# From step 28 on, the FFN's products on TensorE in a fixed order by pairs of steps

## The chip, the cores and the metric

One core of one Trainium2 chip runs the whole program. The metric is device time in microseconds; before, three runs gave a median of 957.44 us (956.3 to 957.57).

## What is computed

Attention of 8 batches, 8 heads, 576 positions and 64 channels, made of a coarse part and a narrow band, and then a feed-forward block over all 4608 tokens:

```python
x = np.ascontiguousarray(attn_out.transpose(0, 2, 1, 3)).reshape(B * S, H * D)   # 4608 x 512
h = x @ w_in                       # 512 x 2048
r = np.maximum(h, 0.0)
g = s * (r * r) + b
return (g @ w_out).astype(np.float32)   # 2048 x 512
```

The attention itself adds two softmaxes: `out_d`, of queries, keys and values averaged over groups of 4 positions, repeated 4 times, and `out_local`, where a position sees only those less than 4 away.

## The kernel before

**Tiles and steps of the FFN.** The tokens are cut into 18 blocks `t` of 256, the 2048 hidden channels into 8 pieces `p` of 256. A step is one pair `(t, p)`; the list `order` (L784 to L787) has all 144 of them. From index 24 on it goes block by block: `(3, 0)` to `(3, 7)`, then `(4, 0)` and so on. Step 28 is `(3, 4)`, step 143 is `(17, 7)`.

Operands are split into a high and a low part of type fp32r, and a product takes three matmuls: high by high, low by high, high by low. One step has

- 24 products with w_in (`products1`, L631): the weights `wi` are loaded into the array, `xh` and `xl` stream past, 256 columns each, into the PSUM bank `ph`. Even steps use bank 4, odd ones bank 6 from block 3 on (but for step 25);
- `upper` (L644 to L646) on ScalarE: Relu and Square in place in `ph`, then a cast to `gh`;
- `lower` (L651) on VectorE: `gl = ph - gh`. Then `ph` is free again;
- 12 products with w_out (`products2`, L705 to L707): `gh` or `gl` is loaded, `wo` streams past, 512 columns each. Six go into one bank, six into another; from block 3 on these are banks 0 and 1. The third of every three reads `gl`.

`gh` and `gl` have two buffers; from block 3 on a step with `p % 3 == 2` takes a buffer of its own, `gb`, instead. Behind a block's last step `evict` (L683) reads both banks on VectorE, scales, adds and stores (`os`), and only then may the next block's w_out products write there.

**Attention beside it.** The batches of attention run while the FFN works on earlier ones. Their products, transposes included (`sa`, `tp`, `tr`, `up`, `ot`), stand on TensorE between those of the FFN, most of their work on VectorE (L539, L558, L559), GpSimd (L537, L559) and ScalarE. `split_x` makes a block's `xh` and `xl` (L612, L613).

**What sets the order.** Up to step 28 a long text, `PLAN`, fixes each engine's order piece by piece; at its end the w_in and the w_out products of steps 0 to 27 are all issued. Behind it a loop (L913 to L925) takes one step after the other: its 24 w_in products, `upper` and `lower` with high priority, a share of attention (`advance`), then w_out products up to three steps back, and another share of attention. These are only priorities: a list scheduler decides what stands where on each engine, and w_out products slide between w_in products as it sees fit. For the first ten steps `behind_plan` keeps everything behind the plan's last instruction on its engine.

Each engine works through its own queue in order, so an instruction that waits holds up all behind it.

Of the kernel before, what the change touches and what calls it, by code (L numbers as in the profile page):

```python
# [20 lines left out]
B, H, S, D = 8, 8, 576, 64  # L21
# [65 lines left out]
def attention_ffn_kernel(ctx, tc, qk, vw_in, vr_in, vdm, qkn, vn, w_in, w_out, s_in, b_in, out):  # L87
    nc = tc.nc
# [21 lines left out]
    def bank(i, shape, name):  # L110
        return ps.tile(shape, F32, tag=f"k{i}", name=name)
# [488 lines left out]
    def split_x(t):  # L600
        tags = ("os", "xl2") if t == 2 else ("xh", "xl")
        xh, xl = (home[tag].tile([P, HP, TB], F32R, tag=tag, name=name)
                  for tag, name in zip(tags, ("xh", "xl")))
        t0 = t * TB
        while t0 < (t + 1) * TB:
            b = t0 // S
            while (b, HP - 1) not in complete:
                next(gen)
            n = min((t + 1) * TB, (b + 1) * S) - t0
            src = xt[b][:, :, t0 - b * S : t0 - b * S + n]  # L610
            dst = slice(t0 - t * TB, t0 - t * TB + n)
            nc.scalar.copy(xh[:, :, dst], src)  # L612
            nc.vector.tensor_tensor(  # L613
                xl[:, :, dst], src, xh[:, :, dst].bitcast(F32), ALU.subtract)
            t0 += n
        xs[t] = (xh, xl)
# [6 lines left out]
    def products1(t, p):  # L623
        xh, xl = xs[t]
        at = 4 if order.index((t, p)) % 2 == 0 else 6 if t >= 3 and (t, p) != (3, 1) else 7 if t == 1 and p < HF else 5
        ph = acc[(t, p)] = bank(at, [P, 2, TB], "ph")
        for j in range(2):
            f = slice(P * j, P * j + P)
            for k in range(NK):
                for s, xk in ((0, xh), (0, xl), (1, xh)):  # L630
                    nc.tensor.matmul(  # L631
                        ph[:, j], wi[p][:, s, k, f], xk[:, k],
                        start=k == 0 and s == 0 and xk is xh, stop=k == NK - 1 and s == 1)
            yield

    def upper(t, p):
# [23 lines left out]
    def add_rows():  # L660
        for p in range(NFP):
            parts = [wo[p][:, i // 2, i % 2].bitcast(F32) for i in range(4)]
            if p == 0:
                nc.vector.tensor_tensor(bias, parts.pop(), parts.pop(), ALU.add)
                yield
            for part in parts:
                nc.vector.tensor_tensor(bias, bias, part, ALU.add)  # L667
                yield
# [8 lines left out]
    def evict(t):  # L677
        if t < 2:
            os_ = xp.tile([P, 2, DM], F32, tag="xh", name="os")
        else:  # L680
            os_ = xp1.tile([P, 2, DM], F32, tag="os", name="os")
        for i in range(2):
            nc.vector.scalar_tensor_tensor(  # L683
                os_[:, i], oacc[t][i], sb_s, bias, ALU.mult, ALU.add)
        nc.sync.dma_start(
            out[TB * t : TB * t + TB, :].rearrange("(m p) c -> p m c", p=P), os_)

    def gemm2(t, p):
        for _ in products2(t, p):
            pass  # L690

    def products2(t, p):
        gh, gl = gt.pop((t, p))
        if p == 0:
            ob = OB.get(t, OB[0])
            oacc[t] = [bank(i, [P, DM], "po") for i in ob]
        po = oacc[t]
        end = t == NB - 1 and p == NFP - 1
        os_ = xp1.tile([P, 2, DM], F32, tag="os", name="os") if end else None
        for m in range(2):  # L700
            ms = slice(P * m, P * m + P)
            for j in range(2):
                first = p == 0 and j == 0
                last = p == NFP - 1 and j == 1
                nc.tensor.matmul(po[m], gh[:, j, ms], wo[p][:, 0, j], start=first, stop=False)  # L705
                nc.tensor.matmul(po[m], gh[:, j, ms], wo[p][:, 1, j], start=False, stop=False)  # L706
                nc.tensor.matmul(po[m], gl[:, j, ms], wo[p][:, 0, j], start=False, stop=last)  # L707
            if end:
                r0 = TB * t + P * m
                for c in (0, DM // 2):  # L710
                    cs = slice(c, c + DM // 2)
                    nc.vector.scalar_tensor_tensor(
                        os_[:, m, cs], po[m][:, cs], sb_s, bias[:, cs], ALU.mult, ALU.add)
                    nc.sync.dma_start(out[r0 : r0 + P, cs], os_[:, m, cs])
            elif p == NFP - 1 and m == 1 and t >= 2:
                evict(t)
            yield
# [13 lines left out]
    tail = {}  # L731
# [19 lines left out]
    def begin_x():  # L751
        for t in range(2):
            xs[t] = tuple(
                xp.tile([P, HP, TB], F32R, tag=tag, name=tag) for tag in ("xh", "xl"))
        for hs in (slice(0, HP - 1), slice(HP - 1, HP)):
            for t in range(2):
                xh, xl = xs[t]
                src = xt[0][:, hs, t * TB : t * TB + TB]
                nc.scalar.copy(xh[:, hs], src)
                yield  # L760
                nc.vector.tensor_tensor(xl[:, hs], src, xh[:, hs].bitcast(F32), ALU.subtract)  # L761
                yield

    def third_x():
        xs[2] = xh, xl = tuple(
            home[tag].tile([P, HP, TB], F32R, tag=tag, name=tag) for tag in ("os", "xl2"))
        for b, src, dst in ((0, slice(2 * TB, S), slice(0, S - 2 * TB)),
                            (1, slice(0, 3 * TB - S), slice(S - 2 * TB, TB))):
            nc.scalar.copy(xh[:, :, dst], xt[b][:, :, src])
            yield  # L770
            nc.vector.tensor_tensor(
                xl[:, :, dst], xt[b][:, :, src], xh[:, :, dst].bitcast(F32), ALU.subtract)
            yield

    def fourth_x():
        xs[3] = xh, xl = tuple(
            xp.tile([P, HP, TB], F32R, tag=tag, name=tag) for tag in ("xh", "xl"))
        src = xt[1][:, :, 3 * TB - S : 4 * TB - S]
        nc.scalar.copy(xh, src)
        yield  # L780
        nc.vector.tensor_tensor(xl, src, xh.bitcast(F32), ALU.subtract)
        yield

    order = [(t, p) for p in range(HF) for t in range(2)]  # L784
    order += [(2, 0), (2, 1)] + [(t, HF) for t in range(2)]
    order += [(2, p) for p in range(2, NFP)]
# [30 lines left out]
    streams = {"x": begin_x(), "y": third_x(), "z": fourth_x(), "b": add_rows()}  # L817
# [21 lines left out]
    plan = PLAN.split()  # L839
# [10 lines left out]
    @contextlib.contextmanager  # L850
    def behind_plan():

        traced = nc.cur_bb.bb.instructions
        last = traced[-1]
        yield
        start = next(k for k in reversed(range(len(traced))) if traced[k] is last) + 1
        for i in traced[start:]:
            if i.engine in ENGINES:
                tc.add_manual_dep(
                    i, tail[i.engine].name,  # L860
                    mybir.DependencyInfo(
                        mybir.DependencyClass.NoSync, mybir.DependencyReason.DATA),
                    reason="behind_plan")

    gone = {kind: plan.count(kind) for kind in "GRVH"}

    def until(kind, count):
        while gone[kind] < count:
            next(streams[kind])
            gone[kind] += 1  # L870


    need = [0, 2 * HF - 3] + [(S * b // TB) * NFP - 3 for b in range(2, B)]
# [24 lines left out]
    def target(st):  # L898
        return sum(
            min(1.0, max(0.0, (st - free[b]) / (need[b] - free[b]))) * NY[b]  # L900
            for b in range(1, B))

    def advance(st):
        nonlocal done
        while done < target(st):
            with tc.high_priority(offset=300 if done < NY[1] else 60 if done < NY[1] + NY[2] else 0):
                if next(gen, "end") == "end":
                    break
            done += 1

    splits = {(t, NFP - 3): t + 1 for t in range(3, NB - 1)}
    begin = 28
    for st in range(begin, len(order)):  # L913
        t, p = order[st]
        with behind_plan() if st < begin + 10 else contextlib.nullcontext():
            until("G", 2 * st + 2)
            with tc.high_priority():
                until("R", st + 1)
                until("V", st + 1)
            advance(st + 0.5)  # L920
            until("H", 2 * (st + 1 - (2 if t < 3 else 3)))
            advance(st + 1)
            if (t, p) in splits:
                split_x(splits[t, p])
    until("H", 2 * len(order))  # L925


def _layout(q, k, v):
# [59 lines left out]
```

## Time and profile before

| | |
|---|---|
| median of three runs | 957.44 us |
| the profiled execution | 957.55 us |
| its span | 955.7 us |
| TensorE busy | 929.5 us |
| VectorE / ScalarE / GpSimd busy | 636.8 / 476.7 / 415.3 us |
| first w_in product of step 28 | 253.31 us after the span's start |
| last w_in product of step 143 | 940.18 us |

In the profile PE is TensorE's matmuls and PEld its weight loads, DVE is VectorE, ACT is ScalarE, POOL is GpSimd. [...] A row of the timeline has the start in us, the duration in us, engine, line, operation, what is written and read, and in brackets the idle time before it and who ended it. "x2" is two instructions in one row.

### The profile page before, as it was taken

The numbers are of one execution on the slowest core, as the hardware profiler recorded it, in microseconds if no ns is written. First come the engines' busy times: TensorE is split into PE (matmuls) and PEld (weight loads), VectorE is DVE, ScalarE is ACT, GpSimd is POOL, SyncE is SP. The second block draws the span as 40 slices with busy tenths as digits, with TensorE's granted clock in tenths as the row PEclk, the third lists the DMA queues.
The fourth block names the chain that finished last, engine by engine and source line by source line (L and its number), as shares of the span: only waits on it lengthen the run. The fifth ranks groups of instructions, "written<-read, shape, count | busy, mean of one in ns | idle before, by whom it ended". The sixth has DMA issues, their size and how long they took to land.

```text
span 955.7 us, 18449 instructions
## 1 busy us (share of the span) xinstructions
PE 929.5 (97%) x7316; PEld 839.0 (88%) x7316; DVE 636.8 (67%) x1134; ACT 476.7 (50%) x1133; POOL 415.3 (43%) x440
## 2 busy tenths in 40 slices
PE   6699999999999999999999999999999999999998
PEld 5588888888898999998999999999899999999997
DVE  9999999845587778887878787878777321112021
ACT  7977774465552636344454544444544333333231
POOL 6401130010587677777777768676776200000000
PEclk9999999999999999999999999999999999999999
DMA  9755413123232323323232323232311000000000
GB/s 335 254 164 187 145 46 118 67 72 102 84 117 89 117 90 110 95 80 117 89 106 80 127 79 126 81 126 79 114 55 44 1 23 2 23 1 23 1 23 22
DMA packets 31749, 86.24 MB, mean 90 GB/s; under 512 B 3248, under 2 KB 7856, under 8 KB 31664
## 3 DMA queue, kind: packets, MB, share of 16 engines
q1 hardware_dynamic: 31664, 85.08, 26.5%
q8 instruction: 57, 0.93, 0.4%
q14 instruction: 28, 0.23, 0.1%
HBM read 75.63 MB, written 9.44 MB: 89 GB/s over the span
## 4 chain that ended last, share of the span: by engine, by line
PE 82%; DVE 10%; POOL 3%; ACT 2%; issue 2%; DMA 1%; DVEq 0%; POOLq 0%; ACTq 0%
PE ph L631 37%; PE po L705 13%; PE po L706 12%; PE po L707 12%; PE sa L342 2%; DVE bias L667 1%; PE up L383 1%; POOL pr L537 1%; PE ot L569 1%; PE ol L479 1%; DVE es L272 1%; DVE es L273 1%; DVE gl L651 1%; PE sl L436 1%; PE up L381 1%
## 5 line engine op out<-in xcount | busy, mean ns | idle before, releaser
L631 PE MATMUL ph<-xh,wi 128*128 128x256 f32 x2176 | 409.6, 282 | 1.3 <-DVE gl L651 1.3
L631 PEld LDWEIGHTS ph<-xh,wi 128*128 128x128 f32 x2176 | 342.6, 189 | 6.8 <-DVE gl L651 1.7
L631 PE MATMUL ph<-xl,wi 128*128 128x256 f32 x1152 | 324.8, 282 | 0.0
L537 POOL TENSOR_TENSOR pr<-lqk 128x576 f32<-128x576 f32 x140 | 199.6, 1450 | 76.8 <-DMA lqk<-in_qkn_dram 54.0
L631 PEld LDWEIGHTS ph<-xl,wi 128*128 128x128 f32 x1152 | 219.4, 190 | 4.4 <-DVE xl L761 0.3
L644 ACT ACTIVATE ph<-ph 128x512 f32<-128x512 f32 x144 | 83.7, 582 | 249.7 <-PE ph L631 244.0
L705 PE MATMUL po<-wo,gh 128*128 128x512 f32 x456 | 181.3, 398 | 2.0 <-DVE os L683 1.7
L706 PE MATMUL po<-wo,gh 128*128 128x512 f32 x456 | 179.4, 393 | 0.0
L707 PE MATMUL po<-wo,gl 128*128 128x512 f32 x456 | 177.6, 391 | 1.1 <-DVE gl L651 1.0
L651 DVE TENSOR_TENSOR gl<-ph,gh 128x512 fp32r<-128x512 f32 x114 | 78.0, 685 | 125.6 <-ACT gh L646 125.4
L559 POOL TENSOR_TENSOR acc<-acc,pv 128x576 f32<-128x576 f32 x80 | 121.6, 1520 | 51.5 <-DVE acc L559 26.7
L539 DVE TENSOR_REDUCE st<-pr 128x9 f32<-128x576 f32 x140 | 105.9, 756 | 30.6 <-POOL pr L537 26.8
L707 PEld LDWEIGHTS po<-wo,gl 128*128 128x128 f32 x456 | 85.7, 188 | 20.0 <-DVE gl L651 2.4
L705 PEld LDWEIGHTS po<-wo,gh 128*128 128x128 f32 x456 | 85.6, 188 | 18.5 <-DVE os L683 2.1
L646 ACT CAST gh<-ph 128x512 fp32r<-128x512 f32 x114 | 66.6, 586 | 65.9 <-PE po L706 60.7
L706 PEld LDWEIGHTS po<-wo,gh 128*128 128x128 f32 x456 | 85.8, 188 | 14.7 <-issue 0.2
L312 POOL TENSOR_TENSOR dq<-vt 80x64 f32<-80x64 f32 x58 | 22.7, 404 | 174.4 <-PE up L383 172.9
L558 DVE TENSOR_TENSOR pv<-lv,st 128x576 f32<-128x576 f32 x120 | 87.0, 748 | 11.9 <-POOL acc L559 11.3
L645 ACT ACTIVATE ph<-ph 128x512 f32<-128x512 f32 x144 | 83.7, 582 | 3.5
L706 PE MATMUL po<-wo,gb 128*128 128x512 f32 x120 | 47.7, 398 | 0.0
L705 PE MATMUL po<-wo,gb 128*128 128x512 f32 x120 | 47.2, 393 | 0.0
L707 PE MATMUL po<-wo,gb 128*128 128x512 f32 x120 | 46.7, 391 | 0.0
(158 smaller groups left out, 1166.9 us busy)
## 6 DMA issues: line engine op xcount, KB each, us to landing
tqk<-in_qk_dram SPq DMA_DIRECT2D x30, 584.0 KB, 3.8
lqk<-in_qkn_dram SPq DMA_DIRECT2D x20, 768.0 KB, 4.3
lv<-in_vn_dram SPq DMA_DIRECT2D x20, 480.0 KB, 3.3
out_dram<-os SPq DMA_DIRECT2D x17, 512.0 KB, 3.1
wst<-in_moe_w_in_dram SPq DMA_DIRECT2D x7, 1024.0 KB, 6.1
wst<-in_moe_w_out_dram SPq DMA_DIRECT2D x7, 1024.0 KB, 5.0
tvd<-in_vdm_dram SPq DMA_DIRECT2D x29, 160.0 KB, 2.5
tvr<-in_vr_dram SPq DMA_DIRECT2D x29, 128.0 KB, 2.9
```

The costliest lines, as they stand in the source:

```text
L537: nc.gpsimd.tensor_tensor(pr, lqk[:, 0:CH], lqk[:, CH + o : 2 * CH + o], ALU.mult)
L539: nc.vector.tensor_reduce(ls[:, :, o], pr, AX.X, ALU.add)
L558: nc.vector.tensor_tensor(pv, lv[:, o : o + CH], w, ALU.mult)
L559: (nc.vector if o % 3 == 1 else nc.gpsimd).tensor_tensor(acc[:, :, h], acc[:, :, h], pv, ALU.add)
L631: nc.tensor.matmul(ph[:, j], wi[p][:, s, k, f], xk[:, k], start=k == 0 and s == 0 and xk is xh, stop=k == NK - 1 and s == 1)
L644: nc.scalar.activation(ph, ph, AF.Relu)
L645: nc.scalar.activation(ph, ph, AF.Square)
L646: nc.scalar.copy(gh, ph)
L651: nc.vector.tensor_tensor(gl, acc.pop((t, p)), gh.bitcast(F32), ALU.subtract)
L705: nc.tensor.matmul(po[m], gh[:, j, ms], wo[p][:, 0, j], start=first, stop=False)
L706: nc.tensor.matmul(po[m], gh[:, j, ms], wo[p][:, 1, j], start=False, stop=False)
L707: nc.tensor.matmul(po[m], gl[:, j, ms], wo[p][:, 0, j], start=False, stop=last)
```

## The change

The w_in products of a step are cut into three pieces (3, 9 and 12 products) and the w_out products into four of 3 each. The loop goes by pairs of steps, an odd one `st` and the even one behind it: 3 w_in products of `st`, 3 w_out products, 21 w_in of `st`, `upper` and `lower` of `st`, 3 w_out, 24 w_in of `st + 1`, `upper` and `lower` of `st + 1`, 18 w_out. The w_out products are those of `st - 1` and `st`. `products` chains each of these products to the one before on TensorE, so that their order is fixed among themselves; attention's products are still placed by the scheduler. The work is the same to the instruction on every engine.

```diff
     def products1(t, p):
...
+                if j == 0 and k == 0 and order.index((t, p)) > BEGIN:
+                    yield
             yield
...
     def products2(t, p):
...
                 nc.tensor.matmul(po[m], gl[:, j, ms], wo[p][:, 0, j], start=False, stop=last)
+                if j == 0 and order.index((t, p)) >= BEGIN:
+                    yield
...
+    BEGIN = 28
...
-    gone = {kind: plan.count(kind) for kind in "GRVH"}
-
-    def until(kind, count):
-        while gone[kind] < count:
+    chain_end = tail[nc.tensor.engine]
+
+    def products(kind, count):
+
+        nonlocal chain_end
+        for _ in range(count):
+            traced = nc.cur_bb.bb.instructions
+            last = traced[-1]
             next(streams[kind])
-            gone[kind] += 1
+            start = next(k for k in reversed(range(len(traced))) if traced[k] is last) + 1
+            for i in traced[start:]:
+                if i.engine == nc.tensor.engine:
+                    tc.add_manual_dep(
+                        i, chain_end.name,
+                        mybir.DependencyInfo(
+                            mybir.DependencyClass.NoSync, mybir.DependencyReason.DATA),
+                        reason="products")
+                    chain_end = i
+
+    def finish(st):
+        with tc.high_priority():
+            next(streams["R"])
+            next(streams["V"])
+        advance(st + 0.5)
...
-    begin = 28
-    for st in range(begin, len(order)):
-        t, p = order[st]
-        with behind_plan() if st < begin + 10 else contextlib.nullcontext():
-            until("G", 2 * st + 2)
-            with tc.high_priority():
-                until("R", st + 1)
-                until("V", st + 1)
-            advance(st + 0.5)
-            until("H", 2 * (st + 1 - (2 if t < 3 else 3)))
-            advance(st + 1)
-            if (t, p) in splits:
-                split_x(splits[t, p])
-    until("H", 2 * len(order))
+
+    def split(st):
+        if order[st] in splits:
+            split_x(splits[order[st]])
+
+    with behind_plan():
+        products("G", 2)
+        finish(BEGIN)
+        advance(BEGIN + 1)
+    for st in range(BEGIN + 1, len(order) - 1, 2):
+        with behind_plan() if st < BEGIN + 10 else contextlib.nullcontext():
+            products("G", 1)
+            products("H", 1)
+            products("G", 2)
+            finish(st)
+            products("H", 1)
+            advance(st + 1)
+            split(st)
+            products("G", 3)
+            finish(st + 1)
+            products("H", 6)
+            advance(st + 2)
+            split(st + 1)
+    products("G", 3)
+    finish(len(order) - 1)
+    products("H", 8)
```

`G` is the stream of w_in pieces, `R` is `upper`, `V` is `lower`, `H` the stream of w_out pieces.

TensorE where step 28 ends and step 29 begins. Before, the last product of step 28 (the first of the two in row 1005) is followed by all 24 of step 29 (row 1007 and on; the last of them are rows 1020 and 1021), and only then come the first w_out products of step 28:

```order
1005 L631 MATMUL ph<-xh,wi 128x256 x2
1006 L631 MATMUL ph<-xl,wi 128x256
1007 L631 MATMUL ph<-xh,wi 128x256 x2
...
1020 L631 MATMUL ph<-xl,wi 128x256
1021 L631 MATMUL ph<-xh,wi 128x256
1022 L705 MATMUL po<-wo,gh 128x512
1023 L706 MATMUL po<-wo,gh 128x512
```

And now:

```order
1005 L631 MATMUL ph<-xh,wi 128x256 x2
1006 L631 MATMUL ph<-xl,wi 128x256
1007 L631 MATMUL ph<-xh,wi 128x256
1008 L707 MATMUL po<-wo,gh 128x512
1009 L708 MATMUL po<-wo,gh 128x512
1010 L709 MATMUL po<-wo,gl 128x512
1011 L631 MATMUL ph<-xh,wi 128x256
1012 L631 MATMUL ph<-xl,wi 128x256
```

Three w_out products of step 28 moved from behind step 29's w_in products to behind the first three of them. Two lines that the diff adds in `products1` shift the w_out products' lines by two.

ScalarE at the same place: Relu, Square and cast of step 28 are rows 257, 259 and 261. Before:

```order
257 L644 ACTIVATE ph<-ph 128x512
258 L346 ACTIVATE dmx<-dmx 96x3
259 L645 ACTIVATE ph<-ph 128x512
260 L348 ACTIVATE pd,dsm<-sa,dmx 96x144 x3
261 L646 CAST gh<-ph 128x512
262 L352 ACTIVATE dsm<-dsm,eps 96x3
263 L644 ACTIVATE ph<-ph 128x512
```

And now:

```order
257 L646 ACTIVATE ph<-ph 128x512
258 L346 ACTIVATE dmx<-dmx 96x3
259 L647 ACTIVATE ph<-ph 128x512
260 L348 ACTIVATE pd,dsm<-sa,dmx 96x144 x3
261 L648 CAST gh<-ph 128x512
262 L352 ACTIVATE dsm<-dsm,eps 96x3
263 L357 ACTIVATE pd<-pd,dsm 96x144 x3
```

Up to row 262 nothing moved; VectorE's queue is the same as well up to its subtraction of step 28. Behind it attention's L357 now stands ahead of step 29's Relu.

TensorE at the border of two steps near the end, where no attention is left. Before, at the end of the nine w_out products behind step 138:

```order
4319 L705 MATMUL po<-wo,gh 128x512
4320 L706 MATMUL po<-wo,gh 128x512
4321 L707 MATMUL po<-wo,gl 128x512
4322 L631 MATMUL ph<-xh,wi 128x256
4323 L631 MATMUL ph<-xl,wi 128x256
4324 L631 MATMUL ph<-xh,wi 128x256 x2
```

And now, where the pair (139, 140) begins:

```order
4414 L707 MATMUL po<-wo,gh 128x512
4415 L708 MATMUL po<-wo,gh 128x512
4416 L709 MATMUL po<-wo,gl 128x512
4417 L631 MATMUL ph<-xh,wi 128x256
4418 L631 MATMUL ph<-xl,wi 128x256
4419 L631 MATMUL ph<-xh,wi 128x256
4420 L707 MATMUL po<-wo,gb 128x512
4421 L708 MATMUL po<-wo,gb 128x512
4422 L709 MATMUL po<-wo,gb 128x512
4423 L631 MATMUL ph<-xh,wi 128x256
4424 L631 MATMUL ph<-xl,wi 128x256
```

Before, this w_out run of 9 (others have 3 to 24) is followed by a full run of 24 w_in products; now 3 w_in, 3 w_out and 21 w_in products follow a w_out run of 18.

## The prediction

> **What bounds the kernel now.** I read the page's totals first, then the waits of TensorE from step 28 on (250 us to the end; the columns are us in total, times, longest us), then its timeline.
>
> ```profile
> span 955.7 us, 18449 instructions
> PE 929.5 (97%) x7316; PEld 839.0 (88%) x7316; DVE 636.8 (67%) x1134; ACT 476.7 (50%) x1133; POOL 415.3 (43%) x440
> PE po L705 <- DVE os L683: 1.7, 1, 1.7
> PE ph L631 <- DVE gl L651: 1.3, 2, 0.7
> PE po L705 <- ACT gh L646: 0.3, 1, 0.3
> ```
>
> TensorE is the bound, and in the 700 us that the change touches it waits 3.3 us in all. An order can therefore win at most those 3.3 us from waits. Whatever else it wins must come from the spacing of products that wait for nothing. So the timeline is read by distances between starts (us, duration, engine, line). A row x2 holds two products, the second about 0.12 us after the first.
>
> ```profile
> 784.73 0.28 PE L631 MATMUL ph<-xl,wi 128*128 128x256 f32 x1
> ...
> 786.50 0.28 PE L631 MATMUL ph<-xl,wi 128*128 128x256 f32 x1
> ...
> 786.73 0.40 PE L705 MATMUL po<-wo,gh 128*128 128x512 f32 x1
> 786.97 0.40 PE L706 MATMUL po<-wo,gh 128*128 128x512 f32 x1
> 787.20 0.39 PE L707 MATMUL po<-wo,gl 128*128 128x512 f32 x1
> 787.43 0.28 PE L631 MATMUL ph<-xh,wi 128*128 128x256 f32 x1
> 787.55 0.28 PE L631 MATMUL ph<-xl,wi 128*128 128x256 f32 x1
> ...
> 789.93 0.28 PE L631 MATMUL ph<-xl,wi 128*128 128x256 f32 x1
> ...
> 790.15 0.40 PE L705 MATMUL po<-wo,gh 128*128 128x512 f32 x1
> ...
> 791.32 0.39 PE L707 MATMUL po<-wo,gl 128*128 128x512 f32 x1
> ...
> 863.88 0.39 PE L705 MATMUL po<-wo,gh 128*128 128x512 f32 x1
> ...
> 867.96 0.28 PE L631 MATMUL ph<-xh,wi 128*128 128x256 f32 x1
> ```
>
> The w_in product has two speeds. Between 784.73 and 786.50 lie 15 of them, 1.77 us: 118 ns each. Between 787.55 and 789.93 lie 21, 2.38 us: 113 ns each. Shape, tiles and clock are the same; what differs is the run of w_out products ahead. I went through all runs of 24 that follow an unbroken run of w_out and a full w_in run: behind 3 w_out products (four cases, 786.73 is the first) and 5 (one case) they are fast, behind 7 or more they are slow, with no exception. The w_out products show the other side. Undisturbed, 18 of them take 863.88 to 867.96, 227 ns each, but the first five behind any w_in run take 790.15 to 791.32, 1.17 us in place of 1.13. A w_out run thus passes through a transient of five products, 0.03 us long in all; w_in products are slow if it was run to its end and fast if it was cut off. Why, the trace doesn't say.
>
> **Part by part.** Before, nearly every run is 24 w_in, 9 to 24 w_out: transient finished, w_in slow. The two rows below are the first and last w_in product of steps 28 to 143 (2,784 of them). Of the 2,646 distances from one to the next, 1,908 are slow, 8.65 us above 113.3 ns each.
>
> ```profile
> 253.31 0.28 PE L631 MATMUL ph<-xh,wi 128*128 128x256 f32 x1
> 940.18 0.28 PE L631 MATMUL ph<-xh,wi 128*128 128x256 f32 x1
> ```
>
> *w_in spacing.* Of a pair's 48 products now only the first 3 follow a long w_out run (18); the 21 and the 24 follow a run of 3. Slow remain 3 in each of 57 pairs, 48 in the first and last step, and about 90 behind attention's transposes, where the trace has both speeds: 310 by 4.4 ns, 1.4 us. Term: 1.4 − 8.65 = **−7.25**, between −8.65 and 0 (every run stays slow). I take it near the fast end because those five cases agree. None of them has a run of only 3 w_in ahead of the w_out products.
>
> [...]
>
> *w_out spacing.* Per pair one full transient (28 ns) and two cut after three (786.73 to 787.43, 0.70 us for 0.68, 21 ns): 70 ns by 57 pairs, 4.0 us, and 0.4 where attention cuts in. Before, the same excess, summed over w_out neighbours, is 2.9. Term **+1.5**, between 0 and 2.
>
> *A wait added at step 28.* The plan ends with all w_out products of steps 0 to 27 issued. So the pair (29, 30) puts step 28's first three w_out products behind only 3 w_in products of step 29. What they read:
>
> ```profile
> 256.74 0.39 PE L631 MATMUL ph<-xh,wi 128*128 128x256 f32 x2
> 257.05 0.58 ACT L644 ACTIVATE ph<-ph 128x512 f32<-128x512 f32 x1 [0.50 <-PE ph L631]
> 257.85 0.58 ACT L645 ACTIVATE ph<-ph 128x512 f32<-128x512 f32 x1
> 259.42 0.57 ACT L646 CAST gh<-ph 128x512 fp32r<-128x512 f32 x1
> 260.03 0.69 DVE L651 TENSOR_TENSOR gl<-ph,gh 128x512 fp32r<-128x512 f32 x1
> 260.05 0.50 PE L705 MATMUL po<-wo,gh 128*128 128x512 f32 x1 [0.32 <-ACT gh L646]
> ```
>
> Step 28's last w_in product starts at 256.74; the three of step 29 would end their issue at 257.20. gh is ready at 260.05, gl at 260.74. ScalarE and VectorE stand in the same order up to there, so the times hold. Before, 24 w_in products fill this; now TensorE stands 2.85 us, and 0.2 more for gl. Everything on its queue waits behind it. Less the 0.5 lost there before (0.32 of it shown as idle): **+2.6**.
>
> *The clock behind that wait.* Three windows (busy us of PE, PEld, DVE, ACT, POOL, then granted clock):
>
> ```profile
> 45.70:49.10 3.40, 1.50 (x56) 1.29 (x55) 3.40 (x7) 2.91 (x7) 0.00 (x0) 1.00 0.43 108
> 49.10:52.50 3.40, 3.39 (x16) 3.10 (x15) 3.33 (x9) 2.22 (x10) 0.00 (x0) 0.50 0.56 214
> 287.90:291.40 3.50, 1.81 (x9) 1.17 (x8) 3.09 (x10) 2.36 (x5) 1.60 (x5) 1.00 0.89 276
> ```
>
> A stretch with TensorE 44% busy is followed by 3.4 us at half clock; one with 52% isn't. A wait of 2.85 us leaves a stretch of 3.4 us 16% to 58% busy, as it falls. Between 0 and 1.7 us (half of 3.4); I take **+1.7**, nearest to the first row.
>
> [...]
>
> *Waits that go.* w_out now lags its w_in by one step instead of two to three, so gh buffers come free early; TensorE's waits for gl in w_in (1.3) and the one for os (1.7, at 288 us, where w_out products of the next block met a late os) lose their cause: **−3.0**, between −3.3 and 0.
>
> *Waits that may come.* The shorter lag takes cover from the chain Relu, Square, cast, subtract. Unhindered it takes:
>
> ```profile
> 915.26 0.40 PE L705 MATMUL po<-wo,gh 128*128 128x512 f32 x1
> 915.46 0.58 ACT L644 ACTIVATE ph<-ph 128x512 f32<-128x512 f32 x1 [2.41 <-PE ph L631]
> 916.07 0.58 ACT L645 ACTIVATE ph<-ph 128x512 f32<-128x512 f32 x1
> 916.69 0.59 ACT L646 CAST gb<-ph 128x512 fp32r<-128x512 f32 x1
> 917.31 0.69 DVE L651 TENSOR_TENSOR gb<-ph,gb 128x512 fp32r<-128x512 f32 x1 [3.32 <-ACT gb L646]
> 434.51 0.58 ACT L646 CAST gh<-ph 128x512 fp32r<-128x512 f32 x1 [0.94 <-PE po L706]
> 435.74 0.74 DVE L683 SCALAR_TENSOR_TENSOR os<-po,sb_s,bias 128x512 f32<-128x512 f32 x1
> 437.72 0.68 DVE L651 TENSOR_TENSOR gl<-ph,gh 128x512 fp32r<-128x512 f32 x1
> 253.30:740.00 486.70, 483.38 (x3277) 443.39 (x3276) 385.33 (x698) 235.56 (x608) 355.21 (x326) 1.00 0.28 94
> 740.00:940.00 200.00, 200.00 (x1302) 182.50 (x1301) 40.74 (x61) 65.69 (x112) 5.75 (x4) 1.00 0.03 11
> ```
>
> From 915.26 (w_in run over) to 918.00: 2.74 us. gl is first needed by the third w_out product: behind 18 w_out, 3 w_in and 2 w_out (4.1 + 0.35 + 0.45 = 4.9 us) for a pair's second step, behind 3, 24 and 8 (0.7 + 2.7 + 1.85 = 5.25) for its first. So 2.1 and 2.5 us of slack, where two steps' work stood before. From 740 on VectorE is 20% busy and the slack is ample. Until 740 it is 79% busy, and gl then starts up to 2.1 us after the cast ended (435.09 to 437.72 is the worst of a block, 2.6). Some of these exceed the slack by 0.3 to 0.5. At the ten block ends with VectorE busy, os (0.74) must leave bank 0 between the twelfth product of the 18 and the third w_in product behind: 1.36 + 0.35 us for 0.2 + 0.74, so 0.7 of slack. Between 0 and 8 us (0.2 in each of 40 pairs); I take **+2.5**, a wait of 0.06 us a pair, since most gl start at once.
>
> The profiled execution took 957.55 us (span and 1.85 around it; 0.1 above the median of the three runs): 957.55 − 7.25 + 1.5 + 2.6 + 1.7 − 3.0 + 2.5 = **955.6 us**.
>
> **The rivals.** *B, the waits stay away*: clock untouched, no new wait: 955.6 − 1.7 − 2.5 = 951.4. For it: before, TensorE met attention's results without waiting. Against: the 44% row. *C, the product chain becomes the limit*: in the attention part gl is late in most pairs, as in the 437.72 row. At 0.2 us in 40 pairs 8 us instead of 2.5: 961. It decides the sign from 0.16 us a pair, where the sum reaches 959.4. For it: the slack is 2.1 and the worst delay 2.6. Against: VectorE is idle a fifth of that time, and a delay of 2.6 comes once in a block of eight steps. *D, the spacing doesn't follow*: 3 w_in products are too few to start a new transient, the 3 w_out behind them run at 227 ns and the rest stays slow, or attention's products, which stand at 64 places in the products' order against 60, set the speed: 955.6 + 7.25 − 1.5 = 961.4. The change would then not do what its order is able to.
>
> **How the numbers follow.** Forecast 0.50, around 955.6 by 2.3 either way; B 0.20; C 0.18; D 0.12. A measurement tells 0.2% of 957.44, 1.9 us, from no change: 955.5 and 959.4 are the borders. Faster: half of the forecast (0.24) and B, 0.44. Same: the other half (0.25), a third of C, a quarter of D, 0.34. Slower: 0.22. The range 951 to 961.5 leaves out the lower part of B and the upper of C and D, together 0.2.
>
> **What the profile of after would show.** Right: runs of 21 and 24 w_in products at 113 ns, three at 118, w_out triples at 0.70 us; a wait of 2.8 us at 257 us, with 0.50 clock in the window behind; steps 740 on some 2.8 us shorter. Wrong: the 21 at 118 ns (D), or waits of po for gl repeated through 300 to 740 (C). What would overturn it most is a triple without a transient.

## The result and the profile after

The changed kernel takes **966.16 us** (median of 4 runs, 965.42 to 968.14), the kernel before, on the same chip, 957.27 us: a ratio of 1.0098, with a 95% interval of 1.008 to 1.0116. It is 1% slower. The profiled execution took 966.72 us. The page's totals:

```profile
span 964.9 us, 18378 instructions
PE 929.1 (96%) x7316; PEld 835.9 (87%) x7316; DVE 643.8 (67%) x1134; ACT 480.5 (50%) x1133; POOL 417.3 (43%) x440
```

TensorE is as busy as before; the span grew by 9.2 us. The waits of TensorE from 250 us on (us in total, times, longest us), where before they summed to 3.3 us (in the changed kernel L707 to L709 are the w_out products, L653 gl, L685 os):

```profile
PE po L709 <- DVE gl L653: 5.1, 5, 2.8
PE po L707 <- ACT gh L648: 2.7, 1, 2.7
PE po L707 <- DVE lr L544: 2.1, 1, 2.1
PE po L707 <- DVE st L545: 1.0, 1, 1.0
PE po L707 <- DVE st L542: 0.8, 1, 0.8
PE po L707 <- DVE st L548: 0.2, 1, 0.2
```

Now 11.9 us. The first row is the product chain, the second the wait at step 28. The last four name small instructions of attention that no w_out product reads: a wait for VectorE is put down to what ended last there. All four stand at a block's end, where the first product into a bank waits until os has read it, as the rows at 288 us will show: at each of them TensorE starts 0.15 us after the first os of the block has ended.

The order did what it should to the spacing. The timeline of one pair (start us, duration, engine, line):

```profile
864.53 0.28 PE L631 MATMUL ph<-xh,wi 128*128 128x256 f32 x1
...
864.88 0.40 PE L707 MATMUL po<-wo,gh 128*128 128x512 f32 x1
...
865.58 0.28 PE L631 MATMUL ph<-xh,wi 128*128 128x256 f32 x1
...
867.85 0.28 PE L631 MATMUL ph<-xh,wi 128*128 128x256 f32 x1
...
868.66 0.28 PE L631 MATMUL ph<-xh,wi 128*128 128x256 f32 x1
...
871.27 0.28 PE L631 MATMUL ph<-xh,wi 128*128 128x256 f32 x1
```

The triple of w_out takes 864.88 to 865.58, 0.70 us; the run of 21 has 20 distances in 2.27 us, the run of 24 has 23 in 2.61: both 113.5 ns, while one product's row lasts 0.28 us and so overlaps with the next.

I summed all distances between starts of neighbouring matmuls from step 28 on. The products' own time at 113.3 and 226.7 ns (the mean of the fast distances of each shape before) is 630.8 us in every kernel here; what lies above it, in us (a distance too long by more than 0.135 us counts as a wait; these waits also hold what the view above leaves out under 0.2 us, and the restart):

| part | before | after | difference | predicted |
|---|---|---|---|---|
| w_in spacing | 9.2 | 2.6 | −6.6 | −7.25 |
| w_out spacing | 3.0 | 4.1 | +1.2 | +1.5 |
| around attention's products | 50.6 | 51.8 | +1.15 | 0 |
| waits | 4.1 | 14.4 | +10.3 | +2.1 |
| half clock | 0 | 3.3 | +3.3 | +1.7 |
| all from step 28 | 697.7 | 706.9 | +9.2 | −1.95 |

The spacing gain came and the waits took it back twice over. Of the 14.4 us of waits, 3.0 stand at step 28, 6.2 for gl and 5.1 for os. Where the longest of each come from is read on VectorE. First the block end at 288 us, VectorE and then TensorE (the brackets: idle before, and its releaser):

```profile
285.37 0.76 DVE L539 TENSOR_REDUCE st<-pr 128x9 f32<-128x576 f32 x1
288.10 0.76 DVE L539 TENSOR_REDUCE st<-pr 128x9 f32<-128x576 f32 x1 [1.97 <-POOL pr L537]
288.77 0.68 DVE L653 TENSOR_TENSOR gl<-ph,gh 128x512 fp32r<-128x512 f32 x1
289.37 0.22 DVE L542 TENSOR_TENSOR st<-st,omask 128x63 f32<-128x63 f32 x1
289.50 0.74 DVE L685 SCALAR_TENSOR_TENSOR os<-po,sb_s,bias 128x512 f32<-128x512 f32 x1
288.00 0.28 PE L631 MATMUL ph<-xh,wi 128*128 128x256 f32 x1
290.39 0.47 PE L707 MATMUL po<-wo,gh 128*128 128x512 f32 x1 [2.10 <-DVE lr L544]
```

VectorE had nothing to do for 1.97 us: at the head of its queue stood a reduce of attention's scores that waited for GpSimd's product pr, and what stood behind it started only behind it: gl at 288.77, whose cast had ended at 285.0, and os at 289.50, whose bank had got its last product at 286.2. os started 1.4 us after TensorE had run out of other work. Then the longest wait for gl, at 638 us, ScalarE, VectorE, TensorE:

```profile
634.72 0.59 ACT L648 CAST gh<-ph 128x512 fp32r<-128x512 f32 x1
636.18 0.76 DVE L539 TENSOR_REDUCE st<-pr 128x9 f32<-128x576 f32 x1 [0.66 <-POOL pr L537]
637.57 0.76 DVE L539 TENSOR_REDUCE st<-pr 128x9 f32<-128x576 f32 x1 [0.63 <-POOL pr L537]
638.24 1.76 DVE L613 TENSOR_TENSOR xl<-x,xh 128x1024 fp32r<-128x1024 f32 x1
639.92 0.75 DVE L539 TENSOR_REDUCE st<-pr 128x9 f32<-128x576 f32 x1
640.58 0.67 DVE L653 TENSOR_TENSOR gl<-ph,gh 128x512 fp32r<-128x512 f32 x1
641.31 0.50 PE L709 MATMUL po<-wo,gl 128*128 128x512 f32 x1 [2.83 <-DVE gl L653]
```

The cast ended at 635.31; gl started 5.27 us later, behind three reduces, two of which waited for GpSimd, and the split of the next x block. TensorE stood 3.0 us beyond the usual distance, about 5.27 less the slack of 2.1 to 2.5 that the prediction had worked out.

The clock fell twice (busy us of PE, PEld, DVE, ACT, POOL, then the granted clock):

```profile
257.44:260.85 3.41, 0.75 (x3) 0.33 (x3) 3.17 (x6) 2.70 (x11) 3.41 (x4) 1.00 0.00 0
260.85:264.26 3.41, 3.41 (x15) 3.31 (x16) 2.50 (x8) 1.23 (x4) 1.12 (x1) 0.50 0.37 92
288.16:291.57 3.41, 1.31 (x9) 1.08 (x8) 3.14 (x8) 0.21 (x1) 1.00 (x2) 1.00 0.60 218
291.57:294.98 3.41, 3.41 (x18) 3.41 (x18) 3.27 (x8) 0.00 (x0) 2.46 (x2) 0.50 0.70 255
```

The first is the one predicted behind the wait of step 28, the second stands behind the wait for os at 288 us.

### The profile page after: what moved, and what is told of

The parts are those of the page before. It is cut to its first block, busy times and chain, and to the rows that moved or that the text cites. A ratio compares the mean times of both kernels' runs of the same rounds, so it can differ in the third digit from the quotient of the medians.

```text
span 964.9 us, 18378 instructions
## 1 busy us (share of the span) xinstructions
PE 929.1 (96%) x7316; PEld 835.9 (87%) x7316; DVE 643.8 (67%) x1134; ACT 480.5 (50%) x1133; POOL 417.3 (43%) x440
## 4 chain that ended last, share of the span: by engine, by line
PE 65%; DVE 14%; POOL 10%; issue 4%; DMA 4%; ACT 3%; DVEq 0%; POOLq 0%; SPq 0%; ACTq 0%
PE ph L631 30%; PE po L707 10%; PE po L708 10%; PE po L709 10%; POOL pr L537 6%; DMA tqk<-in_qk_dram 3%; POOL acc L559 3%; DVE st L539 2%; PE sa L342 1%; DVE pv L558 1%; DVE gl L653 1%; DVE bias L669 1%; PE ol L479 1%; DMA lqk<-in_qkn_dram 1%; PE ot L569 1%
## 5 line engine op out<-in xcount | busy, mean ns | idle before, releaser
L631 PE MATMUL ph<-xh,wi 128*128 128x256 f32 x2176 | 419.8, 282 | 0.0
L631 PEld LDWEIGHTS ph<-xh,wi 128*128 128x128 f32 x2176 | 348.5, 190 | 8.4
L537 POOL TENSOR_TENSOR pr<-lqk 128x576 f32<-128x576 f32 x140 | 203.4, 1477 | 92.5 <-DMA lqk<-in_qkn_dram 46.4
L707 PE MATMUL po<-wo,gh 128*128 128x512 f32 x456 | 182.5, 400 | 6.8 <-ACT gh L648 2.7
L709 PE MATMUL po<-wo,gl 128*128 128x512 f32 x456 | 179.7, 394 | 6.3 <-DVE gl L653 6.0
L653 DVE TENSOR_TENSOR gl<-ph,gh 128x512 fp32r<-128x512 f32 x114 | 78.1, 685 | 107.8 <-ACT gh L648 107.1
L559 POOL TENSOR_TENSOR acc<-acc,pv 128x576 f32<-128x576 f32 x80 | 115.0, 1437 | 44.6 <-DVE acc L559 31.2
L539 DVE TENSOR_REDUCE st<-pr 128x9 f32<-128x576 f32 x140 | 105.9, 757 | 40.0 <-POOL pr L537 37.1
L709 PEld LDWEIGHTS po<-wo,gl 128*128 128x128 f32 x456 | 85.8, 188 | 28.8 <-DVE gl L653 10.6
L707 PEld LDWEIGHTS po<-wo,gh 128*128 128x128 f32 x456 | 85.6, 188 | 21.4 <-issue 5.4
L653 DVE TENSOR_TENSOR gb<-ph,gb 128x512 fp32r<-128x512 f32 x30 | 20.6, 686 | 47.0 <-ACT gb L648 46.9
L708 PE MATMUL po<-wo,gb 128*128 128x512 f32 x120 | 47.3, 394 | 0.0
L707 PE MATMUL po<-wo,gb 128*128 128x512 f32 x120 | 47.2, 393 | 0.0
```

Of the source, the lines that this page charges most:

```text
L537: nc.gpsimd.tensor_tensor(pr, lqk[:, 0:CH], lqk[:, CH + o : 2 * CH + o], ALU.mult)
L539: nc.vector.tensor_reduce(ls[:, :, o], pr, AX.X, ALU.add)
L559: (nc.vector if o % 3 == 1 else nc.gpsimd).tensor_tensor(acc[:, :, h], acc[:, :, h], pv, ALU.add)
L631: nc.tensor.matmul(ph[:, j], wi[p][:, s, k, f], xk[:, k], start=k == 0 and s == 0 and xk is xh, stop=k == NK - 1 and s == 1)
L653: nc.vector.tensor_tensor(gl, acc.pop((t, p)), gh.bitcast(F32), ALU.subtract)
```

## The experiments

The theory after the result: with one step of lag w_out has too little cover for the delay that VectorE's queue gives to gl and os. Rivals: the start sets everything off; os is only badly placed in its queue; the fixed order itself costs the time. Ratios are to the kernel before on the same chip, each with its 95% interval; a time without a ratio is of one execution.

**One step more of lag.** The change's pattern with all w_out products a step later:

```diff
+            late = st == BEGIN + 1
             products("G", 1)
-            products("H", 1)
+            products("H", 0 if late else 1)
             products("G", 2)
             finish(st)
-            products("H", 1)
+            products("H", 0 if late else 1)
...
-            products("H", 6)
+            products("H", 4 if late else 6)
...
-    products("H", 8)
+    products("H", 12)
```

> The changed order with every w_out product one step later (the first pair issues only step 28's twelve, the end issues three steps' worth), so that gl is needed 7.9 us or more behind its w_in run instead of 4.9. Theory A (the shorter lag costs the waits, the spacing's gain stands): TensorE's waits for gl and os behind step 28 fall from 11.9 us to under 2, no half clock, w_in mostly at 113 ns; 949 to 953 us. Theory B (the fixed order itself makes TensorE wait, since the scheduler can't slide products any more): waits stay above 8 us, 960 us or more. If only the start wait and its clock window go, 961.

959.52 us, ratio 1.0029 (1.0017 to 1.0042): most of the loss is gone, but not all; the 949 to 953 expected were missed. Its waits from 250 us on:

```profile
PE po L707 <- DVE os L685: 6.3, 6, 2.3
PE ph L631 <- DVE gl L653: 1.5, 2, 1.0
```

No w_out product waits for gl any more, and the start's wait and both windows of half clock are gone. os still waits: with a whole step of shift a block's last product falls into the middle of a run of 18, and the next block's products follow at once, with no w_in products between. It is the block's second os that is late: bank 0 is free 0.7 us or more ahead of its next product at every block end, and TensorE waits for bank 1, six products on. So lag cures gl, and where the block ends in the pattern decides over os.

**os first in VectorE's queue.**

```diff
-                evict(t)
+                with tc.high_priority():
+                    evict(t)
```

> The changed kernel, with the block end's os on VectorE issued with high priority. If os is late because the scheduler put attention's work ahead of it, the six waits of the w_out product behind a block end (5.1 us together) and the half clock at 291 us (1.6) go: about 960. If it is late because what stands ahead of it in the queue (gl behind a reduce that waits for GpSimd) is late itself, priority changes little: 965 to 967.

967.11 us, waits as in the change (gl 5.9, gh 2.7, and 2.1, 1.0, 0.8 for os). Priority moves nothing: every engine's order is the same with it. So this run is the change once more and doesn't test whether an earlier os would help; it does show that one order's waits for gl vary (5.1 and 5.9 us).

**Without GpSimd's products.** VectorE reduces the keys themselves instead of the products pr, so that no reduce waits for GpSimd; the scores of this part of attention are not computed.

```diff
-                pr = two.tile([P, CH, D], F32, tag="pl", name="pr")
-                nc.gpsimd.tensor_tensor(
-                    pr, lqk[:, 0:CH], lqk[:, CH + o : 2 * CH + o], ALU.mult)
-                nc.vector.tensor_reduce(ls[:, :, o], pr, AX.X, ALU.add)
+                nc.vector.tensor_reduce(ls[:, :, o], lqk[:, CH + o : 2 * CH + o], AX.X, ALU.add)
```

> The changed kernel without GpSimd's products of the band scores (L537): VectorE's reduces read the key tile in their place, so the scores are not computed, and VectorE no longer waits for GpSimd there. Theory A (gl and os are late because VectorE's queue is held by a reduce that waits for GpSimd): TensorE's waits behind the start one fall from 9 us to under 2.5, 956 to 958. Theory B (the slack is too short for the chain whatever stands beside it): waits stay, 964 or more.

955.44 us, with the change's order and lag. The waits (line numbers three lower here):

```profile
PE po L704 <- ACT gh L645: 2.6, 1, 2.6
PE po L704 <- DVE os L682: 2.4, 2, 1.5
PE po L706 <- DVE gl L650: 0.3, 1, 0.3
```

VectorE carries the same instructions; only what they wait for is gone. The wait at the start stays, those for gl and os fall from 9.2 to 2.7 us. VectorE's own waits for pr, 37.1 us between 250 and 740 us in the change, are gone, while its reduces take as long as before (757 and 756 ns). So most of the waits come from instructions that wait for GpSimd at the head of VectorE's queue. GpSimd's own load is halved as well, 214 us for 417, and some of VectorE's other instructions run faster beside it (xl 1.33 us for 1.70), which this run doesn't keep apart.

**The order of before with a short lag.** One step of lag, no fixed order:

```diff
-            until("H", 2 * (st + 1 - (2 if t < 3 else 3)))
+            until("H", 2 * st)
```

> The kernel before, with its free order, in which alone the w_out products follow one step behind their w_in products in place of three: the lag of the changed kernel without its runs of three and without its chain. Theory A (the lag costs the waits): 5 to 10 us of waits of w_out products for gl, gh and os, the w_in spacing still mostly 118 ns; 960 to 967. Theory B (the fixed chain costs them): few waits, 956 to 958.

966.39 us, as slow as the change, without its spacing (w_in 10.6 us above the nominal time, where the change has 2.6). The waits in the distances come to some 10 us; the view names gl in w_out four times, 3.2 us, but also attention's own transposes, 4.2 us, and no os. So with a short lag the order of before waits as long, but only the 3.2 us for gl are of the kind that the change shows; why the transposes wait stays open.

**The start alone.** The first pair (29, 30) without its two triples:

```diff
+            late = st == BEGIN + 1
             products("G", 1)
-            products("H", 1)
+            products("H", 0 if late else 1)
...
-            products("H", 1)
+            products("H", 0 if late else 1)
...
-            products("H", 6)
+            products("H", 8 if late else 6)
```

> The change with its first pair (29, 30) alone altered: step 28's w_out products all behind the pair's second run of w_in, 24 in one piece; from the pair (31, 32) on the change's own order and lag. Theory (the start costs its wait and one window of half clock, 2.5 + 1.7 us, and the other waits have a cause of their own): the 2.7 us wait for gh and the half clock behind it go, gl's and os's waits stay near 9 us, 961 to 963; 1.7 us less where the wait for os near 288 us no longer leaves one stretch of 3.4 us mostly idle. Rival (the wait at the start shifts attention's work against the products, and the later waits follow from it): the later waits fall below 5 us too, 954 to 958.

963.98 us, ratio 1.0073 (1.0055 to 1.009), 1 us above what the theory had said. The wait for gh and the half clock behind it are gone, but gl alone now waits 8.8 us, and the clock falls at two other places (385.7 us, to 0.50 for 3.41 us behind a stretch with TensorE 32% busy, and 638.3 us). The start is not what sets the rest off.

**os in halves**, on top of the extra step of lag: each half of os issued behind its own six products, with priority.

```diff
...
-        for i in range(2):
+        for i in half:
...
+            elif p == NFP - 1 and t >= 3:
+                with tc.high_priority():
+                    evict(t, (m,))
...
```

> The order of e1_lag, with os issued for each half of a block as soon as its six last products are issued, with high priority, so that bank 0 is read while 24 w_in products run. If the six waits for os (6.3 us) come from os standing late in VectorE's queue, they fall below 1.5 us: 952 to 954. If VectorE is too far behind in any case, they stay: 957 to 959.

958.2 us, ratio 1.0022 (1.0012 to 1.0033). The waits for os remain, 6.1 us in six. VectorE and TensorE at one block end:

```profile
435.62 0.74 DVE L688 SCALAR_TENSOR_TENSOR os<-po,sb_s,bias 128x512 f32<-128x512 f32 x1
...
439.26 1.48 DVE L559 TENSOR_TENSOR acc<-acc,pv 128x576 f32<-128x576 f32 x1
440.78 0.75 DVE L558 TENSOR_TENSOR pv<-lv,st 128x576 f32<-128x576 f32 x1
441.45 0.74 DVE L688 SCALAR_TENSOR_TENSOR os<-po,sb_s,bias 128x512 f32<-128x512 f32 x1
442.25 0.50 PE L711 MATMUL po<-wo,gh 128*128 128x512 f32 x1 [1.11 <-DVE os L688]
```

The first half is early, as it was without the halves too; the second stands behind attention's sums on VectorE, and its bank is needed six products after the first, 1.36 us.

**By single steps, two steps behind.** 1 w_in, 1 w_out, 23 w_in, 11 w_out, always of the step two before; where a block begins, no cut:

```diff
...
+    for st in range(BEGIN + 1, len(order)):
+        cut = 1 if st >= BEGIN + 2 and order[st - 2][1] > 0 else 0
...
             products("G", 1)
-            products("H", 1)
+            products("H", cut)
             products("G", 2)
             finish(st)
-            products("H", 1)
+            if st >= BEGIN + 2:
+                products("H", 3 - cut)
...
```

> A fixed order by single steps that keeps the w_out products two steps behind: 1 w_in, 1 w_out, 23 w_in, 11 w_out, and at the first step of a block 24 w_in, 12 w_out, so that os has a full w_in run of cover. Theory A (the spacing follows a single cut, the waits follow the lag): 7 of 8 runs of 23 at 113 ns, waits behind step 28 below 2 us, no half clock: 949 to 952. Theory B (a fixed chain costs waits whatever its lag): over 957.

954.72 us, ratio 0.9979 (0.9969 to 0.9988): 0.2% faster than before, though not the 949 to 952 expected. No w_out product waits; 4.1 us of waits are left, 2.4 of them attention's transposes.

**The same without the cut**: 24 w_in, then 12 w_out.

```diff
-        cut = 1 if st >= BEGIN + 2 and order[st - 2][1] > 0 else 0
+        cut = 0
```

> The fixed order by single steps without the cut: 24 w_in, then 12 w_out of two steps before, always. It differs from the version by single steps (954.7, 0.21% below before) by the one w_out product in the middle alone. Theory (the spacing of the w_in products is worth about 6 us by itself, and is set by what stood ahead of them): the w_in products go back to 118 ns, the waits stay near 4 us, and the time is 959.5 to 961.5. Rival (the gain came from fixing the order and the lag, not from the spacing): within 1 us of the version by single steps, 954 to 956.

959.06 us, ratio 1.0033 (1.0021 to 1.0045). The w_in products have their longer spacing again, 10.3 us above nominal instead of 3.4. So the spacing by itself is worth 6.9 us of w_in distances, less 0.75 of w_out. Fixing the order at this lag gains nothing by itself.

**The length of the cut.** In the steps from 109 on, where attention is over, each pair of the change has another lead and cut (the table holds leads of 0, 1, 2, 3, 6 and cuts of 0 to 8):

```diff
...
+    PROBE = 109
+    RUNS = ((3, 3, 3), (3, 1, 1), (3, 2, 2), (3, 4, 4), (3, 5, 5), (3, 6, 6), (3, 7, 7), (1, 3, 3), (2, 3, 3),
+            (1, 1, 1), (1, 2, 2), (6, 3, 3), (2, 2, 2), (3, 8, 8), (1, 1, 2), (3, 3, 0), (0, 0, 3))
...
+            if st >= PROBE:
+                lead, cut, more = RUNS[(st - PROBE) // 2]
+                whole, rest = 24, 24 - cut - more
...
```

> The changed kernel; only the attention-free pairs from step 109 on have other run lengths (lead w_in, cut w_out, the rest of the 24 w_in, a second cut of w_out, 24 w_in, the rest of w_out), one pattern a pair: it reads the spacing rule by itself. Theory A (a w_out run of five or fewer is cut off in its transient): w_in runs behind 1 to 5 w_out products at 113 ns, behind 6 or more at 118; a lead of 1 or 2 w_in products starts a new transient as 3 do. Theory B (it takes a certain number, 3 for instance, and a lead of 3): cuts of 1 and 2 or leads of 1 and 2 leave 118 ns. The time is about the changed kernel's, 966, by 2 us either way.

972.46 us, which says nothing, since the long cuts take lag away too. The timeline does:

```profile
804.67 0.40 PE L714 MATMUL po<-wo,gb 128*128 128x512 f32 x1
...
805.60 0.28 PE L631 MATMUL ph<-xh,wi 128*128 128x256 f32 x1
...
808.31 0.28 PE L631 MATMUL ph<-xh,wi 128*128 128x256 f32 x1
...
937.07 0.28 PE L631 MATMUL ph<-xh,wi 128*128 128x256 f32 x1
...
942.05 0.28 PE L631 MATMUL ph<-xh,wi 128*128 128x256 f32 x1
```

Behind four w_out products (804.67 to 805.60) the 24 w_in products have 23 distances in 2.71 us, 118 ns. Behind a run of three, 45 of them have 44 distances in 4.98 us, 113 ns to the last of them. Over all pairs, runs behind 1, 2, 3 and 5 w_out products had 113 ns (behind 1 and 5 after a few longer distances), behind 4, 6 and 7 118 ns; a lead of one w_in product is enough to start afresh. Behind 8 the first run had 118 ns and the second, whose eight products had waits among them, 113. Theory A is wrong at four, and theory B at 1 and 2.

**Half a step more of lag.** The change's pattern, w_out six products later, so that a block ends ahead of the run of 18 and os has a run of 24 w_in products, 2.7 us, as cover:

```diff
+            late = st == BEGIN + 1
             products("G", 1)
-            products("H", 1)
+            products("H", 0 if late else 1)
             products("G", 2)
             finish(st)
-            products("H", 1)
+            products("H", 0 if late else 1)
...
-    products("H", 8)
+    products("H", 10)
```

> The change's own pattern (3, 3, 21, 3, 24, 18), with the w_out products half a step (6 products) later than in the change: the end of a block's po then falls ahead of the run of 18 and behind a whole w_in step, so that the eviction os has the 2.7 us of 24 w_in products ahead of the next use of bank 0, and gl has some 3.8 us more. Theory (w_out's lag is the cover for VectorE's queue, and both gl and os need about 2.3 to 3 us of it): the os waits fall from 6.3 in the version one step later to below 1.5 and gl's stay at zero, no half clock, the w_in products keep their spacing: 952.0 to 953.5. Rival (os is late by VectorE's queue whatever stands ahead of the bank's next use, since the queue itself follows the products): os waits of 4 us or more stay, 957 to 959.

**950.87 us, ratio 0.9946 (0.9934 to 0.9958)**: the fastest of all, 0.54% below before, a little under what was expected. The start's wait and the half clock are gone with the rest. All waits of TensorE from 250 us on:

```profile
PE ph L631 <- DVE gl L653: 1.0, 1, 1.0
PE tp L365 <- ACT pd L357: 0.9, 1, 0.9
```

One block end, VectorE and then TensorE:

```profile
433.77 0.74 DVE L685 SCALAR_TENSOR_TENSOR os<-po,sb_s,bias 128x512 f32<-128x512 f32 x1
435.41 0.76 DVE L539 TENSOR_REDUCE st<-pr 128x9 f32<-128x576 f32 x1 [0.23 <-POOL pr L537]
436.79 0.76 DVE L539 TENSOR_REDUCE st<-pr 128x9 f32<-128x576 f32 x1 [0.62 <-POOL pr L537]
437.45 0.74 DVE L685 SCALAR_TENSOR_TENSOR os<-po,sb_s,bias 128x512 f32<-128x512 f32 x1
437.33 0.40 PE L707 MATMUL po<-wo,gh 128*128 128x512 f32 x1
438.72 0.39 PE L707 MATMUL po<-wo,gh 128*128 128x512 f32 x1
```

The second os still stands behind reduces that wait for GpSimd, 3.7 us behind the first. It no longer matters: bank 0 was free 2.8 us ahead of 437.33, bank 1 half a microsecond ahead of 438.72.

**Cuts of one, and os in halves**: 1, 1, 23, 1, 24, 22 by two steps, with a lag near that of half a step.

```diff
...
-            products("H", 1)
-            products("G", 2)
+            products("H", 0 if late else 1)
+            products("G", 23)
...
-            products("H", 6)
+            products("H", 22)
...
```

> Cuts of one w_out product in place of three (1 w_in, 1 w_out, 23 w_in, 1 w_out, 24 w_in, 22 w_out by two steps), the lag near that of the half-step version, and each half of os issued as soon as its own bank's products are done. Theory (one w_out product behind the lead starts the same spacing of 113 ns, and os in halves starts the first bank earlier): w_in spacing as in the change, waits below 3 us, 950 to 953. Rival (os in halves waits behind VectorE's other work as it did in the version with halves and a step of lag, 6.1 us): 955.5 to 958.

954.18 us, ratio 0.9976 (0.9965 to 0.9986), above the range expected: os is no longer among the waits, but gl is, 3.0 us at two places (1.7 the longest), and the w_in products are a little slower (3.4 us above nominal instead of 2.6).

## Why the prediction was wrong

The forecast was 955.6 us and its range ended at 961.5; the result lies above both. The same distances from step 28 on show which term moved in the kernels that matter (us):

| kernel | w_in | w_out | attention | waits | half clock | all |
|---|---|---|---|---|---|---|
| before | 9.2 | 3.0 | 50.6 | 4.1 | 0 | 697.7 |
| the change | 2.6 | 4.1 | 51.8 | 14.4 | 3.3 | 706.9 |
| half a step more of lag | 2.6 | 3.9 | 50.6 | 2.7 | 0 | 690.6 |
| single steps | 3.4 | 3.7 | 51.2 | 5.7 | 0 | 694.7 |
| single steps, no cut | 10.3 | 2.9 | 50.4 | 4.0 | 0 | 698.4 |

*w_in spacing*: right in size, −6.6 for −7.25. Three w_in products were enough to start a new transient (the triple behind them takes 0.70 us, the 21 behind it 113.5 ns each), so rival D is out. That a run is fast whenever the w_out run ahead was cut off within five products is not right: behind four it was slow where the length of the cut was varied. The change used three, which the cases before had shown.

The kernel before, the change and the run with other lengths each have two spacings for the one shape, 113 and 118 ns, and the single-step order with and without its cut differs by them: 3.4 and 10.3 us above nominal.

*w_out spacing*: right, +1.2 for +1.5. The check that steps 740 on would be some 2.8 us shorter held nearly: the w_in distances there fell by 2.9 us, and the w_out distances grew from 0.9 to 1.3 us above nominal.

*A wait added at step 28*: right in place and size: the idle is 2.7 us, and the distances grew by 2.5, for +2.6.

*The clock behind that wait*: right there, and missed elsewhere. The window behind it had 0.50, but a second one followed the wait for os at 288 us: +3.3 instead of +1.7. The row behind the term, a stretch 44% busy, held for the two of the change, 22% and 38% busy; that other waits would be long enough to do the same was not counted.

*Waits that go*: half right. The two waits of w_in for gl, 1.8 us in the distances, are gone. The wait for os at 288 us is not: at the end of the same block TensorE loses 2.3 us where it lost 1.85. Behind bank 0's last product stood six w_out products before, now six w_out and three w_in, 0.35 us more; but os started 3.3 us behind it where it had started 2.7.

*Waits that may come*: **this is the step that failed.** I took +2.5, "a wait of 0.06 us a pair, since most gl start at once"; the waits for gl and os beside the start's came to 11.3 us (6.2 and 5.1), 9.5 without the one that stood at 288 us before, and beyond the 8 that I had as the upper bound either way. The mechanism for gl stood in the text, as rival C, though its 961 us was too low as well, and the slack was right (2.1 to 2.5 us for gl, 0.7 for os). What was wrong is the delay set against it.

For os I set none, and the trace of before had it. Where nothing stands ahead of it (the block ends from 777 us on), os starts 0.43 us after the start of its bank's last product; at the ten block ends until 740 us it was 0.4 to 2.8 us. The latest of these, whose os stands in the prediction:

```profile
432.90 0.39 PE L707 MATMUL po<-wo,gl 128*128 128x512 f32 x1
435.74 0.74 DVE L683 SCALAR_TENSOR_TENSOR os<-po,sb_s,bias 128x512 f32<-128x512 f32 x1
```

Seven of the ten are later than 0.43 and the slack of 0.76 (0.7 in the prediction) allow, by 6.0 us in sum, near the 5.1 that the change then lost there.

For gl I took the worst delay of before, 2.6 us, and treated it as given. Set against the slack, the delays of before would have cost 0.7 us; the change lost 6.2. Measured from the end of a cast to the start of its gl, for the steps from 28 on until 740 us:

| kernel | steps | mean us | over 2 us | longest us |
|---|---|---|---|---|
| before | 79 | 0.78 | 6 | 2.63 |
| the change | 76 | 1.07 | 12 | 5.28 |
| without GpSimd's products | 78 | 0.52 | 3 | 2.62 |
| half a step more of lag | 79 | 1.50 | 19 | 4.53 |
| single steps | 79 | 2.06 | 41 | 4.26 |

For gl the delay is no property of the kernel before: with the products moved, attention's instructions fall differently among VectorE's, and the longest delay doubled. The two faster kernels have longer mean delays than the change and hardly wait: their slack is larger. For steps 29 to 103 the first product that reads a step's gl starts at least 6.7 us (half a step) and 11.5 us (single steps) after the step's last w_in product, in the change at least 5.0. And the cost isn't the same in each pair, as "0.2 us in each of 40 pairs" had it: some six waits for gl and six for os, up to 3 us each, make it up, and two of the waits in all cost clock besides. An average of idle time (VectorE idle a fifth of the stretch) says nothing about those: at 288 us VectorE was idle and os still late.

*Not in the sum*: 1.15 us around attention's products. Half a step more of lag has the same pattern and 50.6 us there, as before, so it is not the pattern's own; which instruction loses it was not found. Nor is it settled why the single steps without a cut are 2.7 us slower than before by their medians, where their profiled distances differ by 0.7 us alone.

## What to carry to other kernels

The steps by which w_out lags its producers are cover for the longest delay in the queue between them, here VectorE's, so work out the slack of each reader, and set it against delays of several times the mean (5.28 us at a mean of 1.07 for gl in the change), since moving the work reshuffles that queue (the longest was 2.63 before). A gain in spacing and a loss of cover can come in one change and be taken apart: here the pattern was worth some 5 to 6 us of distances, and half a step of lag turned 1% slower into 0.5% faster. Some of the delays can be read before the change (os here), others come with the new order (gl here). Where a bank changes hands, choose the place in the pattern at which other work stands ahead of its next use.

## What was not expected of the hardware

The spacing of a w_in run is not a matter of a short w_out run alone: in the run with other lengths it is 113 ns behind 5 products and 118 behind 4 or 6. Nor does the number decide. Before, at 261.08 us, 24 w_in products behind four w_out products that had waited for gh have 113 ns; and in the order of before with a short lag, 23 of them behind six w_out products with a single w_in product ahead of those have 113 ns three times (at 790.39 us first). What sets the spacing stays open.

A wait's length did not decide whether it cost clock. In the version with one step more of lag TensorE stood 2.5 us at 291 us, longer than the change at 288 us, and kept its clock. In the change the granted clock falls to 0.50 at 45.81, 260.85 and 291.57 us and is 1.00 again from 52.63, 264.26 and 294.98 on: each of these is a multiple of 3.41 us from the others. On a grid of that step, laid in the version with more lag by its own changes of clock, the wait falls into two stretches:

```profile
289.14:292.55 3.41, 2.30 (x11) 1.55 (x9) 2.93 (x10) 2.27 (x5) 1.57 (x5) 1.00 0.89 296
292.55:295.97 3.42, 2.19 (x11) 1.89 (x12) 3.42 (x5) 0.00 (x0) 2.73 (x3) 1.00 0.45 168
```

Each is about 65% busy in TensorE, and the clock stays 1.00; in the change the wait at 288 us fell into one stretch, 38% busy with 2.1 idle us, and cost the next one half its clock. Nor does the busy share of a stretch decide alone: before, TensorE is 34% busy from 25.19 to 28.60 us (1.17 of 3.41 us), and the clock stays 1.00 there and in the next 3.42 us. What does is not shown.
